# The second layer's gate as one Silu operation, in a kernel of attention and two gated layers

## The chip, the cores and the metric

The kernel runs on one core of one Trainium2 chip. The metric is the device time of one execution in microseconds, the median of three runs. In the text PE is TensorE (matmuls), PEld its weight loads, DVE is VectorE, ACT is ScalarE, POOL is GpSimd, and SP is the queue that issues the DMAs.

## The reference

The program is an attention over 32 memory slots, followed by two layers with a gate. Only the two layers matter here (4608 tokens, width 512, inner width 2048, all float32):

```python
def _moe_ref(x, w_in, w_out):
    h = x @ w_in
    g = h * (1.0 / (1.0 + np.exp(-1.702 * h)))
    return g @ w_out

def _moe2_ref(x, w_in, w_out):
    h = x @ w_in
    g = h * (1.0 / (1.0 + np.exp(-h)))
    return g @ w_out
```

The second layer's gate is h times the sigmoid of h. Since 1 + tanh(h/2) is twice the sigmoid of h, the kernel before, which carries half of h through this layer (the output of layer one is scaled by 0.25 where its gate is doubled), gets the same value from (1 + tanh(h/2)) times h/2.

## The kernel before

The work runs in four stages, each bound to one weight matrix. Stage one is the attention with the first layer's first product. Stage two is the first layer's second product (line 516). Stage three is the second layer's first product with its gate (line 604), and stage four its second product (line 676). Every float32 operand is split into a high part, which ACT casts, and a low part, which DVE makes by a subtraction; a product takes three matmul passes (high with high, high with low, low with high). Every matrix product of two by two blocks is made with seven block products in place of eight.

Stage three goes by slots, `step1(n, k)`. There are 48 slots of new work (six blocks of 768 tokens times eight groups of 128 rows of the inner width). A slot has seven steps, k from 0 to 6, and each step issues one block product of six matmuls: at k=0 product 1, at k=1 product 2, at k=3 product 6, at k=5 product 5 and at k=6 product 7 of the new slot n, and at k=2 product 3 and at k=4 product 4 of the slot before. The PSUM tile `xb` of a slot is summed up through products 1, 6, 7 and 4; between them ACT copies the partial sum out (at k=0 into `e1`, line 636; at k=3 into `e2`, line 653), so the next product onto `xb` waits for that copy. Product 5 goes to a tile `y2`, which ACT copies out at k=5 (line 664) before product 3 adds to it. DVE adds the pieces to the four pre-gate sums of a slot (line 61).

The gate of each of the four sums is two operations. `tanh` (lines 611 to 613) is a Tanh on ACT into a tile `gq`; `close` (lines 615 to 620) is a multiply-add on DVE, (gq + 1) times the sum, and the store of the tile to HBM on SP's queue (line 620). Three sums lie in SBUF (tile `e`), the fourth in PSUM (`xb`). `tanh` is issued right behind the DVE addition that makes the sum, and ahead of the copies at k=0 and k=3; `close` follows one step later, except for the sum in PSUM, where both are at k=4.

All instructions of an engine run in the order in which they are issued. Other work of ACT, DVE, POOL and SP is set by hand at (slot, step) and issued behind the step's own (`emit`): the split of the next weights (lines 427 and 430), the loads, conversion and stores of the raw weights (lines 93 to 104, 456), the next block's input (lines 573, 584, 591 and 595), and in the last slots the loads for stage four (`r_fetch`, line 474) and its first operands (`make`, line 499). Two helpers, lines 61 and 64, record all additions and subtractions. Stage four's first operand number 2 is made at step 2 of the tail slot 48, and the last gates of stage three follow it there.

Of the kernel before, what the change touches and what calls it, by code (L numbers as in the profile page):

```python
# [8 lines left out]
F32 = mybir.dt.float32  # L9
# [4 lines left out]
ACTF = mybir.ActivationFunctionType  # L14
ALU = mybir.AluOpType
# [6 lines left out]
def attn_moe_moe(ctx: ExitStack, tc: tile.TileContext, q, k, v, phi, w1i, w1o, w2i, w2o, out):  # L22
    nc = tc.nc
# [10 lines left out]
    HB = 384  # L34
    NBK = NT // (2 * HB)
    scale = 1.0 / float(D) ** 0.5
# [18 lines left out]
    pools = {}  # L55
# [4 lines left out]
    def add(eng, out, a, b):  # L60
        eng.tensor_tensor(out=out, in0=a, in1=b, op=ALU.add)  # L61
# [532 lines left out]
        t = xt[b, i]  # L594
        sub(eng, t[:, :, 1], xr.pop((b, i)), rd(t[:, :, 0]))

    e1, e2, xb, y2, gq = {}, {}, {}, {}, {}

    def prod1(n, i, out, start):
        b, f = divmod(n, 8)  # L600
        w, x, f0 = wt[0, f // 2, i], xt[b, i], (f % 2) * 128
        for s in range(2):
            for n, (wi, xi) in enumerate(PASSES):
                nc.tensor.matmul(out=out, lhsT=w[:, s, wi, f0:f0 + 128], rhs=x[:, s, xi],  # L604
                                 start=(start and s == 0 and n == 0), stop=(s == 1 and n == 2),
                                 skip_group_check=True)

    def e_tile():
        return pools["m3"].tile([128, HB], F32, tag="e", name="e", bufs=6)

    def tanh(key, h):
        t = gq[key] = pools["m3"].tile([128, HB], F32, tag="gq", name="gq", bufs=8)
        nc.scalar.activation(out=t, in_=h, func=ACTF.Tanh)  # L613

    def close(n, i, j, h):
        b, f = divmod(n, 8)
        t = gq.pop((n, i, j))
        nc.vector.scalar_tensor_tensor(out=t, in0=t, scalar=1.0, in1=h, op0=ALU.add, op1=ALU.mult)  # L618
        c0 = (2 * b + j) * HB
        nc.sync.dma_start(out=gs[1][f // 2 + 4 * i][:, f % 2, c0:c0 + HB], in_=t)  # L620

# [2 lines left out]
    def ybuf(n):  # L624
        return pools["psy"].tile([128, 512], F32, tag=f"y{n % 4}", name="y2")[:, :HB]

    def step1(n, k):
        new, old = n < NG1, n > 0
        if k == 0 and new:
            xb[n] = pools["ps3"].tile([128, 512], F32, tag="x", name="xb", bufs=3)[:, :HB]  # L630
            prod1(n, 1, xb[n], True)
            e1[n] = e_tile()
        if k == 0 and old:
            tanh((n - 1, 1, 1), e2[n - 1, 2])
        if k == 0 and new:
            nc.scalar.copy(out=e1[n], in_=xb[n])  # L636
        if k == 0 and old:
            close(n - 1, 1, 1, e2.pop((n - 1, 2)))
        if k == 1 and new:
            y1 = pools["ps3"].tile([128, 512], F32, tag="y1", name="y1")[:, :HB]  # L640
            prod1(n, 2, y1, True)
            add(nc.vector, e1[n], e1[n], y1)
            tanh((n, 0, 0), e1[n])
        if k == 2 and old:
            prod1(n - 1, 3, y2[n - 1], False)
            add(nc.vector, e2[n - 1], e2[n - 1], y2.pop(n - 1))
            tanh((n - 1, 0, 1), e2[n - 1])
        if k == 2 and new:
            close(n, 0, 0, e1.pop(n))
        if k == 3 and new:  # L650
            prod1(n, 6, xb[n], False)
            e2[n] = e_tile()
            nc.scalar.copy(out=e2[n], in_=xb[n])
        if k == 3 and old:
            close(n - 1, 0, 1, e2.pop(n - 1))
        if k == 4 and old:
            prod1(n - 1, 4, xb[n - 1], False)
            tanh((n - 1, 1, 0), xb[n - 1])
            close(n - 1, 1, 0, xb.pop(n - 1))
        if k == 5 and new:  # L660
            y2[n] = ybuf(n)
            prod1(n, 5, y2[n], True)
            e2[n, 2] = e_tile()
            nc.scalar.copy(out=e2[n, 2], in_=y2[n])  # L664
        if k == 6 and new:
            prod1(n, 7, xb[n], False)
            add(nc.vector, e2[n, 2], e2[n, 2], xb[n])
# [351 lines left out]
    for b in range(1, NBK):  # L1019
        n = 8 * b - 8  # L1020
# [7 lines left out]
    n = 7 * (NG1 - 8)  # L1028
# [15 lines left out]
    for n in range(NG1 + 1):  # L1044
        for k in range(7):
            step1(n, k)
            emit(n, k)
# [49 lines left out]
```

## Time and profile before

| what | value |
|---|---|
| median of 3 runs | 1530.3 us (1529.82 to 1533.07) |
| the profiled execution | 1529.22 us, its span 1527.4 us |
| mean granted clock of TensorE over the span | 0.978 |
| PE busy over the span | 1421.2 us (93%) |
| PEld busy | 1335.1 us (87%) |
| DVE busy | 1144.9 us (75%) |
| ACT busy | 787.2 us (52%) |
| stage three, its first and last matmul start | 786.4 and 1156.3 us |
| stage four, its first matmul | 1161.0 us |

Times in the rows are counted from the start of the span. A row of the timeline has start, duration, engine, line, operation, tiles and shapes, the number of instructions merged in it, and in brackets the idle time of the engine before it with what ended that. A matmul's own duration overlaps that of the next one, so the pace of PE is read from the starts and from the idle time of the weight loads; a product of six matmuls takes 1.04 us where nothing waits.

### The profile page before, as it was taken

How to read it: one execution, taken by the hardware profiler on the slowest of the kernel's cores; microseconds unless marked ns; L12 is line 12 of the kernel's file. 1: busy time of each engine (PE TensorE's matmuls, PEld its weight loads, DVE VectorE, ACT ScalarE, POOL GpSimd, SP SyncE). 2: the span in 40 equal slices, each digit the busy share in tenths (PEclk: the TensorE clock that was granted, in tenths of full speed). 3: DMA queues.
4: the chain of work that ended last, by engine and by line, in shares of the span. 5: the costliest groups of instructions: out<-in, count | busy, mean ns of one | idle time of the engine just before them, and what ended most of it. 6: DMA issues, size and time to landing. Idle time of an engine off the chain costs nothing. (4 is left out here: it accounts for less than half of the span.)

```text
span 1527.4 us, 28119 instructions
## 1 busy us (share of the span) xinstructions
PE 1421.2 (93%) x10776; PEld 1335.1 (87%) x10776; DVE 1144.9 (75%) x1705; ACT 787.2 (52%) x1407; POOL 215.9 (14%) x209
## 2 busy tenths in 40 slices
PE   5689989998699999999889999999997999999998
PEld 3468777787699999999878999999997999999998
DVE  5767776776588788878887877777787777777765
ACT  3546656655345454454455665655664444444443
POOL 3433636532101101010000110101000000000000
PEclk8899999999899999999999999999999999999999
DMA  9566877845626636447225556465465515425330
GB/s 313 171 195 217 270 256 221 264 165 182 247 73 212 197 121 231 161 160 238 71 94 169 166 189 212 143 220 181 144 207 181 196 42 177 148 71 197 100 118 32
DMA packets 195303, 265.57 MB, mean 174 GB/s; under 512 B 50528, under 2 KB 158048, under 8 KB 195168
## 3 DMA queue, kind: packets, MB, share of 16 engines
q1 hardware_dynamic: 195168, 263.77, 51.8%
q8 instruction: 84, 1.38, 0.4%
q14 instruction: 51, 0.42, 0.1%
HBM read 159.91 MB, written 102.76 MB: 172 GB/s over the span
## 5 line engine op out<-in xcount | busy, mean ns | idle before, releaser
L516 PE MATMUL p<-op,wq 128*128 128x384 f32 x2016 | 365.8, 341 | 28.1 <-ACT op L499 16.9
L516 PEld LDWEIGHTS p<-op,wq 128*128 128x128 f32 x2016 | 353.6, 190 | 40.1 <-DVE op L64 20.4
L676 PE MATMUL p<-wq,op 128*128 128x256 f32 x3024 | 361.2, 283 | 5.2 <-DVE gq L618 4.3
L676 PEld LDWEIGHTS p<-wq,op 128*128 128x128 f32 x3024 | 360.8, 191 | 5.7 <-DVE gq L618 4.6
L499 ACT CAST op<-rr 128x768 fp32r<-128x768 f32 x216 | 178.2, 834 | 200.3 <-PE p L676 77.4
L64 DVE TENSOR_TENSOR op<-rr,op 128x768 fp32r<-128x768 f32 x216 | 209.9, 975 | 94.0 <-ACT op L499 78.5
L321 PEld LDWEIGHTS h<-attnT,slab 128*128 128x128 f32 x1536 | 215.9, 194 | 51.2 <-issue 21.9
L321 PE MATMUL h<-attnT,slab 128*128 128x288 f32 x1536 | 247.2, 311 | 14.3 <-DVE g L327 6.4
L604 PE MATMUL xb<-xq,wq 128*128 128x384 f32 x1152 | 220.5, 340 | 11.1 <-ACT e L636 4.3
L604 PEld LDWEIGHTS xb<-xq,wq 128*128 128x128 f32 x1152 | 201.7, 189 | 17.0 <-ACT e L636 5.6
L327 DVE SCALAR_TENSOR_TENSOR g<-g,h 128x288 f32<-128x288 f32 x256 | 110.7, 445 | 99.2 <-ACT g L326 98.5
L604 PE MATMUL y<-xq,wq 128*128 128x384 f32 x864 | 166.6, 337 | 1.2 <-ACT e L664 0.7
L64 DVE TENSOR_TENSOR op<-r,op 128x768 fp32r<-128x768 f32 x120 | 116.7, 975 | 60.2 <-ACT op L499 59.9
L499 ACT CAST op<-r 128x768 fp32r<-128x768 f32 x120 | 99.7, 834 | 108.5 <-PE p L676 43.9
L604 PEld LDWEIGHTS y<-xq,wq 128*128 128x128 f32 x864 | 151.7, 188 | 2.1 <-ACT e L664 1.0
L326 ACT ACTIVATE g<-h 128x288 f32<-128x288 f32 x256 | 102.4, 418 | 91.2 <-PE h L321 71.9
L613 ACT ACTIVATE gq<-e 128x384 f32<-128x384 f32 x144 | 75.5, 524 | 105.2 <-DVE e L61 102.5
L618 DVE SCALAR_TENSOR_TENSOR gq<-gq,e 128x384 f32<-128x384 f32 x144 | 93.8, 657 | 27.4 <-ACT gq L613 24.0
L104 POOL TENSOR_TENSOR wst<-wst 128x512 int32<-128x512 int32 x24 | 34.5, 1438 | 507.7 <-DVE wst L102 264.9
L427 ACT CAST wq<-wst 128x512 fp32r<-128x512 f32 x83 | 51.2, 619 | 44.1 <-DVE wst L64 25.5
L61 DVE TENSOR_TENSOR e<-e,y 128x384 f32<-128x384 f32 x96 | 52.3, 550 | 16.5 <-PE y L604 13.5
L240 PE MATMUL aa<-w,kvT 64*32 64x512 f32 x496 | 40.7, 619 | 12.7 <-POOL w L104 6.4
(118 smaller groups left out, 1313.9 us busy)
## 6 DMA issues: line engine op xcount, KB each, us to landing
rr<-gs SPq DMA_DIRECT2D x120, 384.0 KB, 6.5
gs<-g SPq DMA_DIRECT2D x128, 288.0 KB, 4.3
gs<-gq SPq DMA_DIRECT2D x192, 192.0 KB, 2.2
r<-gs SPq DMA_DIRECT2D x72, 384.0 KB, 5.5
xs<-o SPq DMA_DIRECT2D x24, 384.0 KB, 4.7
xr<-xs SPq DMA_DIRECT2D x24, 384.0 KB, 4.5
out_dram<-o SPq DMA_DIRECT2D x24, 384.0 KB, 2.6
rawe<-in_moe_w_in_dram SPq DMA_DIRECT2D x16, 512.0 KB, 6.7
```

Of the source, the lines that this page charges most:

```text
L61: eng.tensor_tensor(out=out, in0=a, in1=b, op=ALU.add)
L64: eng.tensor_tensor(out=out, in0=a, in1=b, op=ALU.subtract)
L321: nc.tensor.matmul(out=h, lhsT=slab[b, f // 4, g][:, wi, f0:f0 + 128], rhs=x[:, g, xi], start=(g == 0 and n == 0), stop=(g == 1 and n == 2))
L326: nc.scalar.activation(out=t, in_=h, func=ACTF.Tanh, scale=0.851)
L327: nc.vector.scalar_tensor_tensor(out=t, in0=t, scalar=1.0, in1=h, op0=ALU.add, op1=ALU.mult)
L427: nc.scalar.copy(out=t[:, :, 0], in_=wst[m, c, k])
L499: nc.scalar.copy(out=t[:, :, 0], in_=s)
L516: nc.tensor.matmul(out=out[:, d, :HB], lhsT=w[:, s, wi, d * 128:(d + 1) * 128], rhs=t[:, s, gi], start=(start and p == 0 and s == 0 and n ...
L604: nc.tensor.matmul(out=out, lhsT=w[:, s, wi, f0:f0 + 128], rhs=x[:, s, xi], start=(start and s == 0 and n == 0), stop=(s == 1 and n == 2), ...
L613: nc.scalar.activation(out=t, in_=h, func=ACTF.Tanh)
L618: nc.vector.scalar_tensor_tensor(out=t, in0=t, scalar=1.0, in1=h, op0=ALU.add, op1=ALU.mult)
L676: nc.tensor.matmul(out=out[:, d], lhsT=t[:, u, gi, d * 128:(d + 1) * 128], rhs=w[:, u, wi], start=(start and d != 1 and p == 0 and u == 0 ...
```

## The change

The gate becomes one ACT operation, Silu of twice the sum, into the same kind of tile, and the store follows it. The DVE multiply-add is dropped. The operation stands where `close` stood, which is behind the copies at k=0 and k=3 and one step later than `tanh` did for two of the sums; the store keeps its place on SP's queue. The products, the copies, the additions and everything that `emit` places are as before.

```diff
-    def tanh(key, h):
-        t = gq[key] = pools["m3"].tile([128, HB], F32, tag="gq", name="gq", bufs=8)
-        nc.scalar.activation(out=t, in_=h, func=ACTF.Tanh)
-
-    def close(n, i, j, h):
+    def gate(n, i, j, h):
         b, f = divmod(n, 8)
-        t = gq.pop((n, i, j))
-        nc.vector.scalar_tensor_tensor(out=t, in0=t, scalar=1.0, in1=h, op0=ALU.add, op1=ALU.mult)
+        t = pools["m3"].tile([128, HB], F32, tag="gq", name="gq", bufs=8)
+        nc.scalar.activation(out=t, in_=h, func=ACTF.Silu, scale=2.0)
         c0 = (2 * b + j) * HB
         nc.sync.dma_start(out=gs[1][f // 2 + 4 * i][:, f % 2, c0:c0 + HB], in_=t)
@@ step1
             e1[n] = e_tile()
-        if k == 0 and old:
-            tanh((n - 1, 1, 1), e2[n - 1, 2])
-        if k == 0 and new:
             nc.scalar.copy(out=e1[n], in_=xb[n])
         if k == 0 and old:
-            close(n - 1, 1, 1, e2.pop((n - 1, 2)))
+            gate(n - 1, 1, 1, e2.pop((n - 1, 2)))
         if k == 1 and new:
             ...
             add(nc.vector, e1[n], e1[n], y1)
-            tanh((n, 0, 0), e1[n])
         if k == 2 and old:
             prod1(n - 1, 3, y2[n - 1], False)
             add(nc.vector, e2[n - 1], e2[n - 1], y2.pop(n - 1))
-            tanh((n - 1, 0, 1), e2[n - 1])
         if k == 2 and new:
-            close(n, 0, 0, e1.pop(n))
+            gate(n, 0, 0, e1.pop(n))
         if k == 3 and new:
             ...
             nc.scalar.copy(out=e2[n], in_=xb[n])
         if k == 3 and old:
-            close(n - 1, 0, 1, e2.pop(n - 1))
+            gate(n - 1, 0, 1, e2.pop(n - 1))
         if k == 4 and old:
             prod1(n - 1, 4, xb[n - 1], False)
-            tanh((n - 1, 1, 0), xb[n - 1])
-            close(n - 1, 1, 0, xb.pop(n - 1))
+            gate(n - 1, 1, 0, xb.pop(n - 1))
```

## Rows read from the trace of the kernel before

**Rows 1.** Busy time, clock and DMA share of stage three and of stage four's start.
```profile
core 0: us, PE busy (x) PEld busy (x) DVE busy (x) ACT busy (x) POOL busy (x), PEclk, DMA share, GB/s
786.00:1161.00 375.00, 358.35 (x2022) 351.30 (x2020) 294.18 (x493) 222.36 (x450) 21.37 (x16) 0.99 0.53 178
1160.00:1170.00 10.00, 9.03 (x55) 9.03 (x56) 4.73 (x7) 3.03 (x4) 0.00 (x0) 0.66 1.04 378
```

**Rows 2.** Waits of the weight loads, 785 to 1165 us: total, times, longest.
```profile
PEld xb L604 <- ACT e L636: 5.6, 4, 3.1
PEld xb L604 <- DVE xq L64: 5.2, 5, 1.2
PEld xb L604 <- ACT e L653: 4.0, 8, 1.1
PEld xb L604 <- DVE e L61: 1.7, 1, 1.7
PEld y L604 <- ACT e L664: 1.0, 1, 1.0
```

**Rows 3.** Timeline around the longest wait in stage three, and one like it later.
```profile
818.65 0.69 DVE L61 TENSOR_TENSOR wst<-wst 128x512 f32<-128x512 f32 x1 [3.43 <-DMA wst<-w2s]
821.17 0.52 ACT L613 ACTIVATE gq<-e 128x384 f32<-128x384 f32 x1 [3.23 <-DVE e L61]
822.12 3.86 PE L604 MATMUL xb<-xq,wq 128*128 128x384 f32 x12 [2.76 <-ACT e L636]
...
1123.40 2.35 PE L604 MATMUL xb<-xq,wq 128*128 128x384 f32 x12 [0.53 <-ACT e L636]
```

**Rows 4.** Timeline of DVE and POOL where two new blocks of input begin.
```profile
855.38 1.31 POOL L104 TENSOR_TENSOR wst<-wst 128x512 int32<-128x512 int32 x1 [13.38 <-DVE wst L102]
855.63 1.48 DVE L618 SCALAR_TENSOR_TENSOR gq<-gq,e 128x384 f32<-128x384 f32 x1
...
1095.74 0.55 DVE L618 SCALAR_TENSOR_TENSOR gq<-gq,e 128x384 f32<-128x384 f32 x1
```

**Rows 5.** Timeline of the end of stage three and the start of stage four.
```profile
1148.44 0.53 ACT L613 ACTIVATE gq<-e 128x384 f32<-128x384 f32 x1 [0.80 <-DVE e L61]
1150.12 0.47 ACT L653 COPY e<-xb 128x384 f32<-128x384 f32 x1
1151.12 0.55 DVE L618 SCALAR_TENSOR_TENSOR gq<-gq,e 128x384 f32<-128x384 f32 x1
1152.11 1.18 SPq L474 DMA_DIRECT2D rr<-gs  x2
1158.18 0.81 ACT L499 CAST op<-rr 128x768 fp32r<-128x768 f32 x1
1160.97 19.57 PEld L676 LDWEIGHTS p<-wq,op 128*128 128x128 f32 x144 [4.65 <-DVE gq L618]
1163.52 2.98 SPq L474 DMA_DIRECT2D r<-gs  x4
1181.63 8.50 PEld L676 LDWEIGHTS p<-wq,op 128*128 128x128 f32 x71 [1.08 <-ACT o L690]
```

**Rows 6.** Groups by line and shape: names, shapes, count, busy us, mean ns, idle before.
```profile
L618 DVE SCALAR_TENSOR_TENSOR gq<-gq,e 128x384 f32<-128x384 f32 x144 | 93.8, 657 | 27.4 <-ACT gq L613 24.0 <-DMA w2s<-wst 0.6
L618 DVE SCALAR_TENSOR_TENSOR gq<-gq,xb 128x384 f32<-128x384 f32 x48 | 26.3, 548 | 6.3 <-ACT gq L613 5.9
L613 ACT ACTIVATE gq<-e 128x384 f32<-128x384 f32 x144 | 75.5, 524 | 105.2 <-DVE e L61 102.5 <-DMA gs<-gq 1.2 <-DMA w2s<-wst 1.2
L326 ACT ACTIVATE g<-h 128x288 f32<-128x288 f32 x256 | 102.4, 418 | 91.2 <-PE h L321 71.9 <-DMA gs<-g 14.8 <-DVE w L101 2.2
L232 ACT COPY qT<-a 128x288 f32<-128x288 f32 x60 | 24.6, 414 | 3.0 <-PE a L228 1.6 <-PE aa L240 1.3
```

**Rows 7.** Timeline: the one table load, and the first gate of stage three.
```profile
3.59 1.28 ACT L186 ACT_TABLE_LOAD   x1 [3.59 <-DMA phi<-in_phi_dram]
...
9.19 1.35 ACT L186 ACTIVATE phi<-phi 128x576 f32<-128x576 f32 x2 [4.31 <-DVE phi L182]
...
791.16 0.53 ACT L613 ACTIVATE gq<-e 128x384 f32<-128x384 f32 x1 [2.26 <-DVE e L61]
```

More of the change, by code (lines that the diff above doesn't have):

```diff
@@ L595, in x_low @@
         sub(eng, t[:, :, 1], xr.pop((b, i)), rd(t[:, :, 0]))
-    e1, e2, xb, y2, gq = {}, {}, {}, {}, {}
+    e1, e2, xb, y2 = {}, {}, {}, {}
     def prod1(n, i, out, start):
```

## The prediction, made before the change was run

> **What bounds the kernel now.** I read the page's busy times first: PE is busy almost throughout, so an engine that is relieved is worth only what PE waits for it. The change lies in stage three alone, so next I took the windows. In the 375 us from 786 to 1161 DVE is busy for 294.2 us (78%) and ACT for 222.4 us (59%) [rows 1]. Neither is full. What counts is who holds PE up, so the third view is the waits of PE's weight loads in this stretch [rows 2]: 5.6 us for the copy at k=0 (line 636), 5.2 us for the low part of a new block's input (line 64), 4.0 us for the copy at k=3 (line 653), 1.7 us and 1.0 us once each. This is the stock from which a gain inside the stage can come, some 17.5 us. Outside it stands the 4.65 us wait at the start of stage four for the last gate [rows 5]. The fourth view, the timeline around single waits, tells what stands ahead of those copies [rows 3 to 5].
>
> **What is removed.** 192 multiply-adds leave DVE: 93.8 + 26.3 = 120.1 us of its 294.2 [rows 6], which leaves about 174 us in the stage (46%). None of it is on PE's own path, so this saving is worth nothing by itself; its worth is in the waits below.
>
> **What is added.** ACT keeps 192 operations, Silu for Tanh. No Silu is in the trace. The nearest rows: Tanh out of PSUM at 128x288 takes 418 ns with a scale, a plain copy of that shape 414 ns [rows 6], so the function hardly enters the price. I take 524 ns for the three sums in SBUF, as Tanh has. As bounds: 20 ns less (a copy is not slower than Tanh) and 0.5 us more, if Silu needed two passes over the data. At the upper bound ACT gets 192 x 0.5 = 96 us more and reaches 318 of 375 us, still below the whole stage; I give it up to 5 us of new PE waits and keep that for the range.
>
> Silu may also need a table that Tanh and Exp did not. The trace has one load, 1.28 us, and it ran 4.3 us ahead of its ACTIVATE, which waited for DVE [rows 7]. The first Silu stands behind a gap of 2.26 us in ACT [rows 7], in which ACT waits for DVE's sum: a load of 1.28 us fits into it, so I count it at nothing. Without that cover it costs up to 1.3 us, once. The Trainium skill's page "ScalarE: Activation LUTs", section "What ACT_TABLE_LOAD costs", speaks against the change here: a switch to another set takes about 2.66 us, a drain included, which would be an estimated 0.4 us more than the gap holds. No row shows such a drain, and the sum would be 0.4 us worse by it.
>
> **What is moved: the copies get ahead of the gates.** Before, Tanh stood ahead of the copies at k=0 and k=3 and waited for a DVE addition, and the copy behind it waited along. The clearest case: DVE stands 3.43 us for a weight DMA, ACT's Tanh waits 3.23 us for DVE's sum, the copy comes after Tanh, and PE waits 2.76 us (3.08 us in weight loads) [rows 2, 3]. After the change the copy needs only PE's product. In this case product 4, one step later, still needs the DVE sum; the sum is done just ahead of 821.17, where Tanh began, and PE would want it at 822.12 - 2.76 + 1.04 (the product between) = 820.4, so I leave 0.7 us of the wait. The twelve matmuls behind that wait took 3.86 us, where twelve behind a short wait took 2.35 [rows 3]; with the shorter wait I expect those 1.5 us back. The other three waits for line 636 are under 0.9 us each, and Tanh with its 0.52 us stood ahead of the copy in each; I count them gone. Together 5.6 - 0.7 + 1.5 = 6.4 us. The same for line 653: of its 4.0 us one wait of 1.1 lies at the stage's end and is counted there; 2.9 us go. The bounds for both: 3 us (the copies find DVE's weight sums ahead of them through ACT's casts instead) and 7.1 + 2.9 = 10.0 us. I take 9.3.
>
> Behind the Silu at k=4, which waits for product 4, the same copy of line 664 is queued as behind Tanh; behind the Silu at k=0 and k=2 the weight casts are queued, as before. The stores on SP keep their place and wait for ACT in place of DVE, one operation less, so loads behind them leave no later.
>
> **New blocks of input.** Of the five waits for line 64 in rows 2 one, of 0.7 us, lies at the stage's start and stays; the other four, 4.5 us in all and 1.1 us each, are one pattern. A POOL addition runs 1.31 us from 855.38, the DVE gate takes 1.48 us instead of 0.55, and the low part of the input comes behind it. The fifth new block, where no POOL addition runs, has a gate of 0.55 us and no wait [rows 4]. Without the gate DVE reaches the subtraction earlier; but POOL may now hold up the subtraction itself. Bounds for one: 0.4 us (POOL ends at 856.69 either way, and the gate held DVE until 857.11) and 1.1 (all). DVE will also have started POOL's input earlier, so I take 0.8, in all 3.2 us (1.6 to 4.5). The Trainium skill, page "SBUF — State Buffer", section "SBUF: two separate sides", says that GpSimd and a VectorE operation with two inputs in SBUF lock each other out for a whole instruction. By that rule the subtraction is the next one locked out, and only 0.4 us would come off each; the 1.48 us agree with it.
>
> **The end of the stage.** ACT's Tanh waits 0.80 us, the copy comes at 1150.12, DVE's gate at 1151.12, and only behind this gate's store does SP issue the loads at 1152.11. They land where ACT casts the operand at 1158.18; behind that cast stand a weight cast and the last gate, and PE begins at 1160.97 [rows 5]. In the new order ACT is 0.8 us earlier, Silu follows the copy at once, and the store needs no DVE operation (about 0.5 us of queue and 0.55 us of its own): the loads leave about 1.9 us earlier, and with an unchanged flight PE begins 1.9 us earlier. The next late thing is the other load, issued at 1163.52 [rows 5]; DVE loses the last two gates ahead of it, so it moves by 1.9 to 2.5 us, and with it the work that PE reaches at 1181.63. I take 2.2 us. The granted clock is 0.66 from 1160 to 1170, that is 1.2 of 2.4 GHz for a part of it, behind a stretch in which PE mostly stood [rows 1]; I count nothing back, because PE would only arrive earlier at the work that waits for that load. Bounds: 0, if the flight is longer by as much, and 5 us, if the gap goes as a whole.
>
> **The sum.** 9.3 + 3.2 + 2.2 = 14.7 us. The profiled execution took 1529.2 us, so it becomes 1514.5. The median is 1.1 us above it, which gives 1515.6; I say 1516.
>
> **The rivals.**
> - *Half of it.* The waits stay with the weight work: ACT's weight casts wait for DVE's sums, those for a DMA, and a copy that overtakes Tanh still stands behind a cast. Then 3 us for the copies, 1.6 for the new blocks, 2 at the end: 6.6 us, 1524. For it: the longest wait began with a DMA [rows 3]. Against it: most waits have Tanh directly ahead of the copy.
> - *Hidden anyway.* PE finds a next late thing each time, and only a microsecond or two stays: 1527.5 to 1532. For it: PE is busy on 358 of 375 us [rows 1]. Against it: the waits in rows 2 are waits of PE itself.
> - *More.* All waits of rows 2 but the start's 0.7 us go, and the end gap with them: 20 us or over, below 1511.
> - *Slower: ACT becomes the bound through its tables.* If Silu's table didn't serve the copies, each slot (copy, two Silu, copy, two Silu, copy) would switch four times, at 1.28 us [rows 7]. A slot has 375/48 = 7.8 us, of which ACT uses 222.4/48 = 4.6; with 5.1 us more it needs 9.7, and 48 slots take 93 us longer: 1620. The point from which it decides is 2.5 loads in a slot. Against it: Exp, Tanh and all kinds of copies ran on one load in the whole trace [rows 7].
>
> **How the numbers follow.** The forecast (1511 to 1520) gets 0.60, half of it (1520 to 1527) 0.20, hidden anyway 0.10, more 0.05, slower 0.05. A measurement of this kernel can tell about 0.2%, 3.1 us, from no change. Faster by more than that is 0.60 + 0.20 + 0.05 = 0.85, the same 0.10, slower 0.05. The range reaches into the half case and down to the upper bounds of the new blocks and the end: 1510 to 1524.
>
> **What would show it.** The DVE group of line 618 gone, DVE at about 174 us in the stage, a Silu of 0.49 to 0.53 us, one more table load near 790 us. PE's waits for the copies of lines 636 and 653 (their new line numbers) nearly gone, those for line 64 at half or less, twelve matmuls near 822 at 2.35 us in place of 3.86. Stage three would end its matmuls some 12 us earlier, and the gap to stage four stay about as it is. The prediction is wrong if Silu takes over 0.6 us, if table loads repeat, or if the copies still wait, now behind a weight cast or a Silu that waits for DVE.

## The result, and the profile after

| | before | after |
|---|---|---|
| median | 1530.5 us (4 runs) | 1514.69 us (4 runs, 1512.86 to 1515.67) |
| ratio | | 0.9892, 95% interval 0.9875 to 0.9909 |
| profiled execution, its span | 1529.22, 1527.4 us | 1512.86, 1511.1 us |
| start of stage three to its product 4 in the last full slot (A) | 361.1 us | 347.0 us |
| from there to the ninth operand of stage four (B) | 34.2 us | 30.8 us |
| from there to the end of the span | 345.8 us | 345.8 us |

The changed kernel is 15.8 us faster; the forecast was 14.5 (1516), the range 1510 to 1524. The lower rows of the table are worked out from the starts of the weight loads in the two traces: A runs from the first load of stage three, B ends with the 145th load of stage four. All of the gain lies in A (14.1 us) and B (3.4 us). The stages ahead of A took 1.0 us longer in the profiled execution of after; nothing of them was changed, and A and B are counted from the stage's own start.

Stage three and the start of stage four, by windows (the columns are those of [rows 1]):

```profile
786.00:1143.00 357.00, 353.58 (x2027) 351.75 (x2025) 197.21 (x301) 224.56 (x451) 21.81 (x16) 1.00 0.55 185
...
1140.00:1150.00 10.00, 7.54 (x48) 7.22 (x49) 7.12 (x10) 6.13 (x11) 0.00 (x0) 0.83 1.04 373
```

DVE falls from 294.2 to 197.2 us, ACT stays (224.6). The granted clock at the border of the stages is 0.83 in its ten microseconds, where it was 0.66.

The waits of the weight loads from 785 to 1155 us (total, times, longest), the answer to [rows 2]:

```profile
PEld p L666 <- ACT gq L614: 2.8, 1, 2.8
PEld y L604 <- DVE xq L64: 0.8, 1, 0.8
PEld xb L604 <- DVE e L61: 0.8, 1, 0.8
PEld xb L604 <- DVE xq L64: 0.7, 1, 0.7
...
PEld y L604 <- ACT e L654: 0.4, 1, 0.4
```

Line 614 is the Silu, 629, 644 and 654 are the copies that were 636, 653 and 664, and 666 is the second product, which was 676. Not one wait for the copies at k=0 and k=3 is left, and of the five for line 64 only the one at the stage's start.

The groups of ACT in the stage (count, busy us, mean ns, idle before):

```profile
L614 ACT ACTIVATE gq<-e 128x384 f32<-128x384 f32 x144 | 75.8, 527 | 15.0 <-DVE e L61 14.8
L614 ACT ACTIVATE gq<-xb 128x384 f32<-128x384 f32 x48 | 23.6, 492 | 3.2 <-ACT gq L614 0.2
...
L614 ACT ACT_TABLE_LOAD x1 | 1.3, 1283 | 0.0
```

Silu costs what Tanh did, 527 ns against 524 [rows 6]. Its wait for DVE's sums is 14.8 us where Tanh's was 102.5: the gate now comes after the copy, when the sum is mostly there. Most of those 102.5 us had never reached PE, whose waits for the two copies were 9.6 us [rows 2].

The timeline around the place of the longest wait, the answer to [rows 3]:

```profile
817.39 0.69 DVE L61 TENSOR_TENSOR wst<-wst 128x512 f32<-128x512 f32 x1 [3.61 <-DMA wst<-w2s]
...
817.67 0.48 ACT L629 COPY e<-xb 128x384 f32<-128x384 f32 x1 [1.01 <-PE xb L604]
...
819.50 2.24 PE L604 MATMUL xb<-xq,wq 128*128 128x384 f32 x12
...
819.91 0.53 ACT L614 ACTIVATE gq<-e 128x384 f32<-128x384 f32 x1 [1.76 <-DVE e L61]
```

DVE stands for the weight DMA as long as before (3.61 us), and the gate waits for DVE. But the copy at 817.67 is ahead of the gate and waits for PE alone, and the twelve matmuls follow without a wait and at full pace, 2.24 us in place of 3.86.

POOL and DVE where a new block begins, the answer to [rows 4]:

```profile
849.70 1.31 POOL L104 TENSOR_TENSOR wst<-wst 128x512 int32<-128x512 int32 x1 [13.17 <-ACT xq L591]
849.95 1.88 DVE L64 TENSOR_TENSOR xq<-xr,xq 128x768 fp32r<-128x768 f32 x1
```

The subtraction that makes the low part is now the one that meets POOL, and takes 1.88 us instead of 0.95; it ends at 851.83, and PE does not wait.

The end of stage three, the answer to [rows 5]:

```profile
1136.41 1.18 SPq L474 DMA_DIRECT2D rr<-gs  x2
...
1141.32 0.83 ACT L499 CAST op<-rr 128x768 fp32r<-128x768 f32 x1
...
1143.59 18.48 PEld L666 LDWEIGHTS p<-wq,op 128*128 128x128 f32 x144 [2.77 <-ACT gq L614]
...
1147.05 3.10 SPq L474 DMA_DIRECT2D r<-gs  x4
...
1153.73 0.96 DVE L61 TENSOR_TENSOR rr<-rr,r 128x768 f32<-128x768 f32 x1 [4.36 <-DMA r<-gs]
...
1165.27 14.91 PEld L666 LDWEIGHTS p<-wq,op 128*128 128x128 f32 x125 [3.20 <-ACT o L680]
```

Stage four starts 4.4 us earlier in B than before, but the wait behind its first 144 matmuls grows from 1.08 to 3.20 us: a part is given back to the loads that leave at 1147.05. The gap ahead of stage four shrinks from 4.65 to 2.77 us.

### The profile page after: what moved, and what is told of

The parts are those of the page before. It is cut to its first block, busy times and chain, and to the rows that moved or that the text cites. A ratio compares the mean times of both kernels' runs of the same rounds, so it can differ in the third digit from the quotient of the medians.

```text
span 1511.1 us, 27760 instructions
## 1 busy us (share of the span) xinstructions
PE 1415.0 (94%) x10776; PEld 1334.0 (88%) x10776; DVE 1046.9 (69%) x1513; ACT 788.8 (52%) x1408; POOL 216.1 (14%) x209
## 4 chain that ended last, share of the span: by engine, by line
PE 69%; DVE 12%; DMA 5%; ACT 5%; issue 4%; POOL 1%; SPq 1%; ACTq 0%; DVEq 0%; POOLq 0%
PE p L666 23%; PE xb L604 13%; PE p L516 12%; PE y L604 10%; PE h L321 8%; DVE op L64 4%; DMA gs<-g 2%; PE aa L240 2%; DVE rr L64 2%; ACT op L499 1%; PE a L196 1%; DMA rr<-gs 1%; DVE o L531 1%; ACT g L326 1%; DVE r L64 1%
## 5 line engine op out<-in xcount | busy, mean ns | idle before, releaser
L604 PE MATMUL xb<-xq,wq 128*128 128x384 f32 x1152 | 216.5, 336 | 0.9 <-DVE e L61 0.5
L614 ACT ACTIVATE gq<-e 128x384 f32<-128x384 f32 x144 | 75.8, 527 | 15.0 <-DVE e L61 14.8
L61 DVE TENSOR_TENSOR e<-e,xb 128x384 f32<-128x384 f32 x48 | 26.6, 554 | 76.7 <-PE xb L604 70.9
L629 ACT COPY e<-xb 128x384 f32<-128x384 f32 x48 | 23.0, 480 | 57.9 <-PE xb L604 57.9
```

What stands on the lines that cost most here:

```text
L614: nc.scalar.activation(out=t, in_=h, func=ACTF.Silu, scale=2.0)
```

## The experiments

The theory at the outset, called *order*: PE waited because Tanh, which waits for DVE, stood ahead of the copies that PE needs; the new place behind the copies is most of the gain. The rival, *DVE load*: Tanh waited because DVE was full, and dropping 192 operations is the gain wherever the gate stands. All ratios are to the kernel before on the same chip. A and B are those of the table above, since the stages ahead differ by some microseconds from execution to execution (stage three began between 782.1 and 790.3 us in the first four profiles).

**Order alone.**

```diff
@@ step1
-        if k == 0 and old:
-            tanh((n - 1, 1, 1), e2[n - 1, 2])
         if k == 0 and new:
             nc.scalar.copy(out=e1[n], in_=xb[n])
+        if k == 0 and old:
+            tanh((n - 1, 1, 1), e2[n - 1, 2])
 ...                            # the others likewise; close one step behind tanh
```

> Order alone: Tanh and the multiply-add stay, but Tanh is issued behind the copies at k=0 and k=3 and one step later for two of the sums, where Silu stands in the changed kernel, and each multiply-add one step behind its Tanh, as before. Theory (order): PE's waits for the copies of lines 636 and 653 came from Tanh standing ahead of them and waiting for DVE; they go (5.6 + 2.9 us and 1.5 us of slow clock, some 10 us), while the four waits of 1.1 us at new blocks and the end gap stay. Time about 1520 to 1522, against 1530.5. Rival (DVE load): Tanh waited because DVE was full, so order matters little: 1527 to 1531, and the waits for the copies stay, now behind a weight cast.

1519.43 us, ratio 0.9933 (0.9921 to 0.9945). A is 350.6 us, 10.5 less than before; B is 32.5. The place of the old longest wait and a new block, in the timeline:

```profile
823.78 1.00 PEld L604 LDWEIGHTS xb<-xq,wq 128*128 128x128 f32 x6 [0.21 <-DVE e L61]
...
854.96 1.31 POOL L104 TENSOR_TENSOR wst<-wst 128x512 int32<-128x512 int32 x1 [12.24 <-DVE wst L102]
855.21 1.88 DVE L64 TENSOR_TENSOR xq<-xr,xq 128x768 fp32r<-128x768 f32 x1
...
857.15 1.87 PEld L604 LDWEIGHTS xb<-xq,wq 128*128 128x128 f32 x11 [0.83 <-DVE xq L64]
```

Close to the theory's number, and far from the rival's. The longest wait is down to the 0.21 us that product 4 waits for the sum; of the short waits for the two copies 1.6 us stay. The new-block waits did not stay at 1.1 us, though: they are 0.83 and three times 0.39, since the gate's multiply-add now comes a step later and the subtraction meets POOL first.

**DVE's relief alone.**

```diff
-        nc.scalar.activation(out=t, in_=h, func=ACTF.Tanh)
+        nc.scalar.activation(out=t, in_=h, func=ACTF.Silu, scale=2.0)
@@ close
-        nc.vector.scalar_tensor_tensor(out=t, in0=t, scalar=1.0, in1=h, op0=ALU.add, op1=ALU.mult)
```

> DVE's relief alone: Silu in place of Tanh and no multiply-add, but Silu stands where Tanh stood, ahead of the copies and right behind the addition that makes the sum; the store stays where it was. Theory (order): the waits at new blocks (4.5 us) and some 3 us at the end go, the longest wait near 820 us stays at about 2 us or over with its slow clock, since it began with a DMA that DVE waited for; a part of the short ones goes: 1519 to 1523. Rival (DVE load): the whole gain is here, 1514 to 1516, and no wait for a copy is left.

1515.93 us, ratio 0.9908 (0.9891 to 0.9925). A is 349.1, B 29.7. The one wait for the copies at k=0 and k=3 that is left, in the timeline:

```profile
822.78 0.52 ACT L613 ACTIVATE gq<-e 128x384 f32<-128x384 f32 x1 [3.26 <-DVE e L61]
823.21 0.46 ACT L635 COPY e<-xb 128x384 f32<-128x384 f32 x1
...
823.72 2.04 PEld L604 LDWEIGHTS xb<-xq,wq 128*128 128x128 f32 x12 [2.04 <-ACT e L635]
```

Each side has a part, and the rival the larger one. The time is the rival's, and can't be told from the changed kernel's (0.9892, 0.9875 to 0.9909): of the 17.5 us that A and B gain there, 16.5 are here, with every gate ahead of its copy as before. The wait that began with a DMA stays, as the order theory said, but without the slower clock (2.04 us of loads for twelve). All the short waits for copies inside the stage are gone with the gates still ahead of them. So the two causes of the short waits stand in a row: a gate ahead of the copy, and a DVE queue that makes this gate wait. Taking either away is enough.

**The change with DVE's load put back.**

```diff
         nc.scalar.activation(out=t, in_=h, func=ACTF.Silu, scale=2.0)
...                             # the zeros, and the gate's 6 tiles
+        d = pools["m3"].tile([128, HB], F32, tag="d", name="d")
+        nc.vector.scalar_tensor_tensor(out=d, in0=st["z"], scalar=1.0, in1=h, op0=ALU.add, op1=ALU.mult)
```

> The changed kernel with DVE's load put back: one multiply-add of the same shape beside each Silu, reading the sum and a tile of zeros and writing a tile that nobody reads (the tiles of the gate are 6 in place of 8 to make room). Theory (order): the waits for the copies stay away, the four new-block waits of about 1 us come back (the multiply-add meets POOL's addition again), and at the end some 2 to 3 us: 1520 to 1523. Rival (DVE load): all comes back, 1528 to 1531.

1519.28 us, ratio 0.9924 (0.9908 to 0.9941). A is 352.5, B 31.2. Waits from 785 us on:

```profile
PEld xb L604 <- DVE xq L64: 3.0, 4, 1.2
...
PEld xb L604 <- ACT e L649: 1.6, 3, 0.8
PEld xb L604 <- ACT e L634: 0.9, 2, 0.5
```

With Silu and the new order, DVE's load alone costs 5.5 us in A: the new-block waits come back with 3.0 us, and a few short waits for copies with 2.5. The bulk does not come back. This agrees with order alone: with DVE's load back, 8.6 us (here) and 10.5 us (order alone) of the 14.1 us of A remain; with the old order back, 12.0 us (DVE's relief alone).

**Tanh for Silu.** The gate is then only a tanh.

```diff
-        nc.scalar.activation(out=t, in_=h, func=ACTF.Silu, scale=2.0)
+        nc.scalar.activation(out=t, in_=h, func=ACTF.Tanh, scale=2.0)
```

> The changed kernel with Tanh in Silu's place, which needs no second table load; the gate is then only a tanh, so that this part of the computation is left out. Theory: Silu costs what Tanh does (0.52 us out of SBUF) and the load lies in a gap of ACT: within 1.5 us of the changed kernel, 1513 to 1516. Rival (the load is paid at the start of the stage, with its drain): faster than the changed kernel by 1.3 to 2.7 us or more, 1512 or below.

1513.66 us, ratio 0.9895 (0.988 to 0.991); A 347.1, B 30.9, each within 0.1 us of the changed kernel. The table load costs nothing. Its place in the changed kernel, in the timeline of ACT:

```profile
789.98 1.28 ACT L614 ACT_TABLE_LOAD   x1
792.20 0.53 ACT L614 ACTIVATE gq<-e 128x384 f32<-128x384 f32 x1 [0.94 <-DVE e L61]
```

It runs ahead of the wait of its ACTIVATE and ends 0.94 us before that is due.

**POOL's addition moved, in the kernel before.**

```diff
-        x = 42 + 14 * n
+        x = 42 + 14 * n + (4 if n in (1, 5, 9, 13) else 0)
```

> The kernel before, with the conversion of four raw weight pieces (the casts on ACT, three DVE and POOL operations, the load and the store) four steps later, so that POOL's addition no longer runs where a new block of input begins. Theory (POOL meets the gate there): the four waits of 1.1 us for line 64 go, 1525 to 1527, against 1530.3. Rival (DVE's queue is too long there whatever POOL does): waits of 0.7 us or over stay, 1529 to 1531.

1528.33 us, ratio 0.9992 (0.998 to 1.0004): no difference that can be told, and between the two forecasts. Waits from 785 to 1170 us:

```profile
PEld xb L604 <- ACT e L636: 7.8, 8, 3.2
...
PEld xb L604 <- ACT e L653: 4.4, 7, 1.2
...
PEld xb L604 <- DVE xq L64: 0.7, 1, 0.7
```

The mechanism is right: the four waits of 4.5 us are gone. The gain was given back: the same work, four steps later, delays DVE's sums there, and the copies behind Tanh wait more (7.8 + 4.4 us where it was 5.6 + 4.0). A falls by only 1.7 us. In the changed kernel no gate stands ahead of a copy to give it back to; that this is why its gain stayed was not run by itself.

**The first layer too.**

```diff
-        nc.scalar.activation(out=t, in_=h, func=ACTF.Tanh, scale=0.851)
-        nc.vector.scalar_tensor_tensor(out=t, in0=t, scalar=1.0, in1=h, op0=ALU.add, op1=ALU.mult)
+        nc.scalar.activation(out=t, in_=h, func=ACTF.Silu, scale=1.702)
@@ quarter, plus
-    0.25
+    0.5 / 1.702
```

> The changed kernel with the first layer's gate made the same way (one Silu of 1.702 times the sum; the factor 2/1.702 goes into the scale of the first layer's output, 0.5/1.702 in place of 0.25). This takes 256 multiply-adds of 0.45 us off DVE in stage one, where PE's weight loads wait 14 us for them, and puts table loads of 1.28 us around each Exp of the attention, some 24 pairs. Theory (ACT has room and four PSUM tiles of slack cover a load): 1505 to 1512. Rival (the loads stand ahead of copies and gates and reach PE): slower than the changed kernel, 1520 or over; more than half of 24 x 2.6 = 62 us would make it slower than the kernel before.

1519.09 us, ratio 0.9939 (0.9923 to 0.9954): slower than the changed kernel, by 4.4 us between the medians, and close to the rival's 1520. The loads, by group, and PE's new waits up to 400 us:

```profile
L326 ACT ACT_TABLE_LOAD x21 | 26.9, 1283 | 0.4
L270 ACT ACT_TABLE_LOAD x14 | 18.0, 1283 | 0.2
...
L186 ACT ACT_TABLE_LOAD x7 | 9.0, 1283 | 3.8 <-DMA phi<-in_phi_dram 3.7
```

```profile
PEld h L321 <- ACT g L326: 33.4, 33, 2.3
PEld a L196 <- ACT qT L232: 15.5, 14, 3.9
PEld aa L240 <- ACT qT L232: 13.0, 10, 2.5
```

42 loads where the changed kernel has two, that is 40 x 1.28 = 51 us of ACT. PE's wait for DVE's gates (14.1 us in the changed kernel) is gone, but 33.4 us of waits for ACT's gates stand in its place, and the waits for ACT's copies of line 232 rise from 9.1 to 30.9 us in all. Not all of that is the tables' doing: a load stands in ACT's queue during the wait or up to 1.5 us ahead of it for 8 of the 33 gate waits (11.3 us) and for 10 of the copy waits (20.1 us); most of the other gate waits are of 0.84 us with no load near. With what fell elsewhere, the weight loads' idle time up to 400 us is 132.4 us where it was 123.2. So a table is not free here, where Exp and Silu alternate and there is no gap ahead of each: a kin of the prediction's slower rival, at a much smaller price.

**Two tries at the border of the stages.** The first converts the last weights five to seven steps earlier, the second leaves them and reorders the loads and the gates of the tail.

```diff
-    spread(1, 3, [n + j for j in (51, 52, 54, 56, 57, 59, 61)])
+    spread(1, 3, [n + j for j in (46, 48, 50, 51, 52, 54, 56)])
-    at1(NG1, 2, make, 1, ROOMS[1], 2)
+    at1(NG1, 4, make, 1, ROOMS[1], 2)
+    for p in range(4):
+        at1(NG1, 2, r_fetch, 1, 0, 3, p)
...                             # these four loads no longer behind the stage
```

> The changed kernel with the last weights of stage four converted five to seven steps earlier, into the room that DVE has gained, the four loads that were issued at 1147 us issued at step 2 of the tail slot, and operand number 2 made behind the last gate. Theory (the gap of 2.8 us at the start of stage four and the wait of 3.2 us behind it hang on DVE's last weight work and on these loads): both shrink to under 1 us each, 1509 to 1512, against 1514.7. Rival (the loads collide with those ahead of them, or the weights land late): no gain, 1514 to 1517.

1516.77 us, ratio 0.9914 (0.99 to 0.9929): not faster. A is 347.7, B 34.0, 3.2 us worse. ACT and PE, in the timeline:

```profile
1142.90 0.62 ACT L427 CAST wq<-wst 128x512 fp32r<-128x512 f32 x1 [1.28 <-PE xb L604]
...
1145.06 1.78 PEld L604 LDWEIGHTS y<-xq,wq 128*128 128x128 f32 x6 [2.70 <-ACT e L654]
...
1147.39 0.62 ACT L427 CAST wq<-wst 128x512 fp32r<-128x512 f32 x1 [2.38 <-PE y L604]
```

The new weights lie in the rooms of the old ones, so an earlier cast waits for PE's last use of them (1.28 and 2.38 us in these rows). Behind the cast at 1142.90 stands the copy of line 664 (654 here), for which PE waits 2.70 us: a wait on PE itself, which neither theory had. PE's other new wait there, 2.54 us for the copy at k=3, has casts ahead of the copy too, but those waited for DVE's weight sums (1.71 us).

```diff
-    at1(NG1, 2, make, 1, ROOMS[1], 2)
+    at1(NG1, 4, make, 1, ROOMS[1], 2)
+    at1(NG1, 3, r_fetch, 1, 0, 3, 1)
+    at1(NG1, 5, r_fetch, 1, 0, 3, 3)
@@ step1
+        if k == 2 and old and n > 46:
+            gate(n - 1, 0, 1, e2.pop(n - 1))
...                             # and not again at k == 3; the other two loads as before
```

> The changed kernel with its tail in another order: one gate of the last full slot and of the tail slot ahead of its copy (so that its store, and the loads behind it on SP, go earlier), two of the four loads that were issued at 1147 us issued in the tail slot as their tiles come free, and operand number 2 made behind the last gate. The weights stay at their old steps. Theory (the order of issue on SP sets when stage four gets its data): the waits of 2.8 and 3.2 us shrink by 2 to 3 us in all, 1512 to 1513.5 against 1514.7. Rival (the DMA engines are full there, 0.99 busy at some 380 GB/s from 1137 to 1155 us, so an earlier issue lands no earlier): 1514 to 1516, with 3 us or over at the second wait.

1516.63 us, ratio 0.9911 (0.9891 to 0.9931): not faster; A 347.0, B 33.4. The late loads and the first sum that needs them, in the timeline:

```profile
1148.54 2.36 SPq L474 DMA_DIRECT2D r<-gs  x3
...
1156.67 0.96 DVE L61 TENSOR_TENSOR rr<-rr,r 128x768 f32<-128x768 f32 x1 [6.06 <-DMA r<-gs]
```

DVE waits 6.06 us for its load, where it waited 4.36. The rival's sign is there: 2.77 us ahead of stage four and 3.49 us at the second wait, and a time just above its 1516. Its reason is shown only in part. The DMA engines are busy at this border, in the changed kernel (share 1.04 from 1140 to 1150 us in the window above) and here (0.96). But of the four loads one left earlier, and the other three, behind it on SP, left 13.8 us after product 4 where all four had begun to leave at 12.6; the sum comes 2.6 us later by the same measure. How much of that is the order on SP and how much the full engines, these runs don't tell. Neither version beats the changed kernel.

**The longest wait alone, in the kernel before.**

```diff
-    spread(0, 3, range(25, 39, 2))
+    spread(0, 3, range(28, 42, 2))
```

> The kernel before with the conversion of one set of weights (steps 25 to 38 of stage three) three steps, 3.1 us, later, so that its DMA has landed when DVE comes to it. Theory (the longest wait of PE, 3.1 us near 820 us, began with that DMA, and the lower clock behind it cost 1.5 us): the wait shrinks to under 0.6 us, twelve matmuls behind it take 2.3 to 2.4 us, and the time falls by 4 us to 1525 to 1527. Rival (Tanh would stand ahead of the copy and wait all the same): a wait of 2 us or over stays, 1529 to 1531.

1531.66 us, ratio 1.0011 (0.9995 to 1.0027): no gain; the rival's time. The timeline of PE, SP and ACT:

```profile
823.89 2.05 PEld L604 LDWEIGHTS xb<-xq,wq 128*128 128x128 f32 x12 [0.83 <-ACT e L653]
...
835.34 0.33 SPq L76 DMA_DIRECT2D wst<-in_moe_w_out_dram  x1
...
839.66 0.66 ACT L93 ACTIVATE wst<-wst 128x512 f32<-128x512 f32 x1 [4.02 <-DMA wst<-in_moe_w_out_dram]
...
842.94 3.39 PEld L604 LDWEIGHTS xb<-xq,wq 128*128 128x128 f32 x12 [4.17 <-ACT e L653]
```

Near 820 us the wait of 3.08 us is gone; one of 0.83 us for the other copy is there, with full pace behind it, much as the theory said. But the raw weights that come next use the tile that the moved conversion frees. They are loaded 48.1 us after the stage's start, as before (48.0), while PE and ACT, without the wait near 820, arrive earlier. So ACT's conversion waits 4.02 us for them where it had waited 1.52, and PE has a wait of 4.17 us at 842.94 for a copy, with slow matmuls behind it (3.39 us of loads for twelve, 2.05 behind the short wait). The wait has moved, and nothing is gained. A DMA that is late costs PE only as long as a copy for PE stands behind those who wait for it: in the changed kernel DVE waits 3.61 us for one, and PE not at all.

## Why the prediction was right, step by step

**What bounds the kernel** held: the gain is the waits of PE, and their stock was read rightly. Every term had the right sign and place, and every one was a little too small. What was wrong in kind was one number (DVE at 174 us), one reading (the stores leaving "no later") and, of more weight, the split between the two causes: DVE's relief alone is worth nearly the whole gain.

**The copies, 9.3 us with the slower clock.** All of the waits went, 10.0 us with the slow matmuls, which was the upper bound. The step that was mis-sized is the 0.7 us left of the longest wait: nothing is left. Before, SP issued the weight DMA 24.1 us after the stage's start and DVE went on at 32.3; after, 22.0 and 30.0 (787.41 is the stage's start there). PE itself is 0.7 us ahead by then; the rest I put down to the stores ahead of the DMA on SP, which no longer wait for a second operation. I had the stores leaving "no later"; they leave earlier.

**New blocks, 3.2 us.** All 4.5 went, again the upper bound. POOL's addition does meet the subtraction now (1.88 us), as the row of the gate had suggested. By the rule of the Trainium skill's "SBUF — State Buffer", section "SBUF: two separate sides", this was to happen, and the trace agrees: the subtractions of line 64 onto `xq` rose from 949 to 1048 ns on average. But the pair runs earlier: POOL's addition starts 2.0 us ahead of the product that needs the low part (product 7), where it was 1.3, and the low part is ready at 851.83, just ahead of PE's load at 851.88 for the matmul that reads it. So the whole wait went, and by a margin of 0.05 us, which is luck. The 0.4 us that the rule alone would have given per block was too low by that, and my 0.8 too.

Together A gained 14.1 us where I had 12.5; the waits that went, 10.0 + 4.5, make 14.5, and 0.4 stays unexplained.

**The end, 2.2 us.** B gained 3.4. The first loads leave 2.7 us earlier counted from the last product 4 (1.9 forecast). The mis-sized step is the other load, which I had named as the next late thing: it leaves 3.5 us earlier (12.6 us after product 4 where it was 16.1), and I had 1.9 to 2.5. B follows it. Stage four starts 4.4 us earlier and its first 144 weight loads take 18.48 us in place of 19.57, but PE then waits 2.1 us longer for that load. So counting nothing for the clock was right: PE only arrives earlier at the wait. The gap ahead of stage four did not stay as it is, as I had written; it fell by 1.9 us.

**The total.** A and B together gained 17.5 us where I had 14.7. That the median still came within 1.3 us of 1516 is luck in part: the stages ahead took 1.0 us longer in the profiled execution, and the median of the changed kernel lies 1.8 us above that execution, where I had added 1.1.

**The table.** One load, in the gap, at no cost, also by the run without it. The 0.4 us that the Trainium skill's page "ScalarE: Activation LUTs", section "What ACT_TABLE_LOAD costs", would have added did not show.

**DVE at 174 us** was wrong: it is 197 us. Some 10 us went into operations that now meet POOL (subtractions of line 64 onto `xq` and `xr`, by mean and count in the two traces: 3.9 and 6.7). The rest I put down, as an estimate, to the overlap of back-to-back operations, since an operation of 0.55 us frees DVE for the next after some 0.47 (before, at 1157.17 and 1157.64): up to 192 x 0.08 = 15 us, and 12.5 are to be explained. So the busy times of dropped operations could not simply be subtracted here.

**How I read the causes** was half right. I ascribed the copies' 9.3 us to the order, called DVE's relief worth nothing by itself, and had no rival in which it does the work. The runs show that order alone gives 10.5 us of A and DVE's relief alone 12.0, both together 14.1; of B they give 1.7, 4.5 and 3.4. They overlap, and the change has a reserve. The forecast would have come out as near with the relief alone (1515.9): its number does not bear out its mechanism. Only the longest wait needs the order, and only the new blocks and the last 1.6 us of short waits need the relief. What stays open is how the two divide the short waits in the changed kernel itself; either suffices, so no run can ascribe them to one.

**The rivals.** Half of it (1524), hidden anyway and more (below 1511) are excluded by the interval, the last only just. Of *more* the first half came true: inside the stage all waits but those at its start and its end went. The end gap did not go with them (2.77 us). The slower rival's repeated loads exist where Exp and Silu alternate, as the first layer showed, but not in stage three, where the copies run on Silu's table: two loads in the whole execution.

## What to carry to other kernels

Read which instruction stands directly ahead of the one that the bounding engine waits for, on its own queue, and what that one waits for: here a gate that nobody needs soon stood ahead of a copy that PE needed at once. There were two ways out, to move the gate or to let what it waits for come sooner, and either gave most of the gain; a run of each alone is what tells. Merging two operations saved 120 us of DVE and gave 16: only what PE had waited for. A merged function from another table was free where the kernel stayed on that table, and not where it alternated. A wait that is removed alone (POOL's addition, the late weights) tends to come up again at the next step, as long as what PE needs still stands behind what waits.

## What the runs showed of the hardware

Between ACTIVATEs of the kernel with Silu in both layers, a table load costs its own 1.28 us and hardly more (timeline of ACT):

```profile
212.05 0.48 ACT L326 ACTIVATE g<-h 128x288 f32<-128x288 f32 x1
212.55 1.28 ACT L270 ACT_TABLE_LOAD   x1
213.84 0.68 ACT L270 ACTIVATE nat<-nat 128x576 f32<-128x576 f32 x1
```

From the end of one ACTIVATE (212.53) to the start of the next (213.84) it is 1.31 us. Of a drain besides the load, as the Trainium skill's page "ScalarE: Activation LUTs", section "What ACT_TABLE_LOAD costs", states it (2.66 us in all), these rows show nothing beyond the ACTIVATE ahead running to its end.

A granted clock of 0.50, that is 1.2 in place of 2.4 GHz, came behind a single wait of 3.1 us (the kernel before) or 4.2 us (weights later), and not behind one of 2.0 us (DVE's relief alone), each in a stretch in which PE had been busy but for short waits. The windows right behind these waits, in this order the kernel before, weights later and DVE's relief alone (the granted clock is the third number from the end):

```profile
822.05:825.40 3.35, 3.28 (x10) 3.28 (x11) 3.22 (x7) 2.03 (x6) 0.00 (x0) 0.50 0.21 67
842.55:845.90 3.35, 2.96 (x9) 2.96 (x10) 3.23 (x5) 1.10 (x3) 0.45 (x1) 0.50 0.33 117
823.70:827.10 3.40, 3.38 (x19) 3.38 (x20) 2.76 (x5) 2.74 (x6) 0.00 (x0) 1.00 0.46 164
```

The waits do not settle it alone. Near 740 us, in stage two, all the profiled executions have the same four waits of PE (0.7, 0.8, 1.6 and 0.8 us, with short products between); in five of the eleven the clock fell behind them, and in the others it did not. Order alone, then the kernel before:

```profile
744.90:748.20 3.30, 3.30 (x12) 3.30 (x12) 2.43 (x4) 0.83 (x1) 0.00 (x0) 0.50 0.38 117
742.10:745.40 3.30, 3.30 (x21) 3.30 (x20) 2.99 (x4) 0.92 (x2) 0.00 (x0) 1.00 0.31 90
```
